# Weight products in one six-bank round and one joined to the scores; the last output tile in two column halves

## Chip, cores, metric

One core of a Trainium2 chip. The metric is the device time of one launch in microseconds (us), as the median of several executions. The profile is one execution with every instruction recorded. The engines are PE (TensorE matmul), PEld (its weight loads), DVE (VectorE), ACT (ScalarE), POOL (GpSimd) and SP (which issues DMAs).

## The reference

Eight batches of eight heads, 576 tokens, head size 64, 32 memory slots. Softmax-weighted sums of keys and values over the tokens give 32 memories per head, each token attends to those 32, and the result, `x` of 4608 x 512, goes through a gated feed-forward block.

```python
k_m = einsum('bhsm,bhsd->bhmd', a, k)        # a = softmax of phi over the tokens
v_m = einsum('bhsm,bhsd->bhmd', a, v)
attn = softmax(q @ k_m^T / sqrt(64))
x = (attn @ v_m), heads side by side          # 4608 x 512
out = (silu(x @ w_gate) * (x @ w_val)) @ w_out   # 512 -> 1536 -> 512
```

## The kernel before

It never forms `x`. It multiplies the value memories with the gate and value weights first: `U = v_m @ W`, per batch two kinds (gate 0, value 1) in three chunks `c` of 512 columns, each in two head groups. Then `x @ W` is `attn @ U`. One batch runs through these stages:

1. `scores` (on PE split into eight tiles of 64 rows x 32 columns, written 64*32), exponentials on ACT, sums and their inverse (`z_inv`), normalised tile `A` on DVE (`norm`);
2. 24 slots `gv_slot`: gate product, silu on ACT, value product, multiplication on DVE;
3. among those slots: output matmuls of the batches before (the "backlog", one unit = one 128x512 matmul), the key/value sums of the next batch (`kv_items`), and rounds of `U`.

In this program a bank is one PSUM buffer of up to 128 x 512 FP32: PE writes a product there, and the bank is free again when ACT or DVE has copied it.

```python
ps = ctx.enter_context(tc.tile_pool(name="ps", bufs=6, space=bass.MemoryType.PSUM))  # general banks
po = ctx.enter_context(tc.tile_pool(name="po", bufs=2, space=bass.MemoryType.PSUM))  # output matmuls

def u_round(b, parts, evac):                   # one bank per kind, chunk and group
    banks = []
    for which, c, halves in parts:
        ...
        for i in range(NP):
            for g in range(NG):
                nc.tensor.matmul(              # 64 rows x 32 columns: 8 tiles at once
                    p[g][32 * i:32 * i + 32, f0:f1],
                    lhsT=kTs[b][64 * g:64 * g + 64, 2, 32 * i:32 * i + 32],
                    rhs=W[which, c][64 * g:64 * g + 64, halves[0]:halves[-1] + 1, i],
                    start=True, stop=True, tile_position=(64 * g, 32 * i))
        ...
    for (t, p), e in zip(banks, evac):         # copies to SBUF: "a" on ACT, "v" on DVE
        ...

for b in range(2, B):                          # cut to what matters
    run(take(2))                               # 2 output matmuls
    for g in range(NG):
        scores(b, g)
    if b == 2:
        load_k(3); load_v(3); load_q(4); load_phi(4, nc.gpsimd)
    run(take(8))
    ...                                        # z_inv, 14 output matmuls, norm
    if b == 2:
        run(take(4))
        run([u_item(2, 0)] + take(6) + [u_item(2, 1)])
    run(take(12))
    # slots, spread over 0..24, with the rest of the backlog, and:
    #   b == 2: ([lambda: load_qT(3)], 12, 12)      q transposed by a DMA on SP
    #   (kv_items(b + 1, lambda: (u_item(b, 2)(), run(take(2)))), 9, 14)
    #   ([u_item(b + 1, 0)], 15, 17)
    #   ([u_item(b + 1, 1)], 21, 23)
    # and the loads, all on POOL's queue, in this order:
    #   load_q(b + 3), load_k(b + 2), load_v(b + 2), load_phi(b + 3)
```

A `u_item(b, c)` is one round of four banks: both kinds of chunk `c`, 16 matmuls in two waves of eight. A round with 128*128 matmuls on both sides is called solo.

The softmax here doesn't subtract the row's maximum and nothing guards it: scores larger than these inputs give would overflow.

Of the kernel before, what the change touches and what calls it, by code (L numbers as in the profile page):

```python
# [9 lines left out]
FP32 = mybir.dt.float32  # L10
# [4 lines left out]
def kernel(  # L15
# [17 lines left out]
    nc = tc.nc  # L33
# [3 lines left out]
    B, H, S, D = q.shape  # L37
    M = phi.shape[3]
    DM, DF = moe_w_gate.shape
# [3 lines left out]
    NJF = DF // 128  # L43
# [11 lines left out]
    work = ctx.enter_context(tc.tile_pool(name="work", bufs=3))  # L55
    ps = ctx.enter_context(tc.tile_pool(name="ps", bufs=6, space=bass.MemoryType.PSUM))
    po = ctx.enter_context(tc.tile_pool(name="po", bufs=2, space=bass.MemoryType.PSUM))
# [3 lines left out]
    out_r = out.rearrange("(b p j) c -> b j p c", b=B, p=P, j=J)  # L61
# [10 lines left out]
    def load_k(b):  # L72
        t = inp.tile([P, 2, H, J * D], BF16, tag="kv", name="t_kv")
        nc.gpsimd.dma_start(out=t[:, 0], in_=k[b].rearrange("h (p j) d -> p h (j d)", p=P))
        kvs[b] = t
# [20 lines left out]
    def load_qT(b):  # L96

        t = att.tile([128, H, 3, P], BF16, tag="qT", name="t_qT")
        nc.sync.dma_start_transpose(
            out=t.rearrange("p h j t -> p (h j) t"),  # L100
            in_=qs[b].rearrange("p h f -> p (h f)"),
        )
        for i in range(NP):
            qTs[b, i] = t[:, 2 * i:2 * i + 2].rearrange("p h j t -> p h (j t)")
# [18 lines left out]
    WO = {}  # L123
# [18 lines left out]
    def phi_exp(b):  # L142
        t = att.tile([P, J, NG, NP, M], BF16, tag="ephi", name="t_ephi")
        src = phis.pop(b).rearrange("p (i g) (j m) -> p g i j m", g=NG, m=M)
        for g in range(NG):
            nc.scalar.activation(  # L146
                out=t[:, :, g].rearrange("p j i m -> p i j m"), in_=src[:, g], func=AF.Exp
            )
        ephis[b] = t
# [201 lines left out]
    def u_round(b, parts, evac):  # L351

        banks = []
        for which, c, halves in parts:
            f0, f1 = HC * halves[0], HC * (halves[-1] + 1)
            p = [ps.tile([128, CH], FP32, tag="b", name=f"p_u{g}") for g in range(NG)]
            for i in range(NP):
                for g in range(NG):
                    nc.tensor.matmul(  # L359
# [3 lines that stand above are left out]
                        start=True,  # L363
                        stop=True,
                        tile_position=(64 * g, 32 * i),
                    )
            for g in range(NG):
                if (b, which, c, g) not in Us:
                    Us[b, which, c, g] = upool.tile(
                        [128, CH], BF16, tag=f"U{which}{c}{g}", name="t_U"  # L370
                    )
                banks.append((Us[b, which, c, g][:, f0:f1], p[g][:, f0:f1]))
        for (t, p), e in zip(banks, evac):
            if e == "a":
                nc.scalar.copy(out=t, in_=p)  # L375
            else:
                nc.vector.tensor_copy(out=t, in_=p)  # L377


    hts = {}  # L380
    pend = []

    def flush_mul():
        while pend:
            pend.pop(0)()
# [44 lines left out]
    def token_segments(t0, count):  # L430
        segs = []
        t = t0
        while t < t0 + count:
            bb, rest = divmod(t, S)
            blk, pp = divmod(rest, P)
            n = min(P - pp, t0 + count - t)
            segs.append((t - t0, n, bb, 2 * (blk % 3) + blk // 3, pp))
            t += n
        return segs

    def out_units(c, u, eng):

        mine = {}

        def unit(jf):
            def run():
                if jf == 0:
                    mine["p"] = po.tile([128, DM], FP32, tag="o", name="p_oo")
                nc.tensor.matmul(  # L449
                    mine["p"],  # L450
                    lhsT=hts[c, jf][:, 128 * u:128 * (u + 1)],
                    rhs=WO[jf],
                    start=(jf == 0),
                    stop=(jf == NJF - 1),
                )
                if jf == NJF - 1:
                    h = DM // 2 if eng == "av" else DM
                    for n, e in enumerate(eng):
                        t_o = work.tile([128, h], FP32, tag="to", name="t_o")
                        c0 = n * h  # L460
                        if e == "a":
                            nc.scalar.copy(out=t_o, in_=mine["p"][:, c0:c0 + h])  # L462
                        else:
                            nc.vector.tensor_copy(out=t_o, in_=mine["p"][:, c0:c0 + h])  # L464
                        q_out = nc.scalar if eng == "av" and e == "a" else nc.sync
                        for (r0, m, bb, jj, pp) in token_segments(2 * c * S + 128 * u, 128):
                            q_out.dma_start(
                                out=out_r[bb, jj, pp:pp + m, c0:c0 + h], in_=t_o[r0:r0 + m, :]
                            )

            return run

        return [unit(jf) for jf in range(NJF)]

    def out_list(b):
        tiles = range(0, 4) if b % 2 == 0 else range(4, 9)
        res = []
        for n, u in enumerate(tiles):
            eng = "av" if b + 1 == B and u == tiles[-1] else "v" if n % 4 != 3 else "a"
            res += out_units(b // 2, u, eng)  # L480
        return res

    def q_items(b, evac):
# [4 lines left out]
    def u_item(b, c, evac="avav"):  # L488

        both = ((0, c, (0, 1)), (1, c, (0, 1)))  # L490
        return lambda: u_round(b, both, evac)
# [6 lines left out]
    def u_half(b, which, c, half, evac):  # L498
        return lambda: u_round(b, ((which, c, (half,)),), evac)

    def run(items):
        for x in items:
            x()
# [10 lines left out]
    def exp_tables():  # L514
        nc.scalar.preload_act_table_set("natural_log_exp_and_others")  # L515
# [102 lines left out]
    def take(n):  # L618
        nonlocal backlog
        n = max(0, min(n, len(backlog)))  # L620
        part, backlog = backlog[:n], backlog[n:]
        return part

    for b in range(2, B):
        last = b + 1 == B
        exp_tables()
        if b == 2:
            load_qT(2)
            phi_exp(2)
            run(take(28))  # L630
            run(kv_items(2)[:1] + take(6) + kv_items(2)[1:] + take(14))
        run(take(2))
        for g in range(NG):
            scores(b, g)
        if b == 2:
            load_k(3)
            load_v(3)
            load_q(4)
            load_phi(4, nc.gpsimd)
        run(take(8))  # L640
        if not last:
            phi_exp(b + 1)
        z_inv(b, 0)
        run(take(1))
        z_inv(b, 1)
        nc.scalar.preload_act_table_set("silu_and_others")
        run(take(13))
        norm(b, 0)
        norm(b, 1)
        if b == 2:  # L650
            run(take(4))
            run([u_item(2, 0)] + take(6) + [u_item(2, 1)])
        run(take(12))
        g = gv_slots(b)
        beside = 0 if last else 2
        outs = [lambda: run(take(1)) for _ in range(len(backlog) - beside)]
        streams = [(g, 0, 24), (outs, 0, 24)]
        if last:
            streams += [([u_item(b, 2)], 5, 6)]
        if b == 2:  # L660
            streams += [
                ([lambda: load_qT(3)], 12, 12),
                (kv_items(3, lambda: (u_item(2, 2)(), run(take(2)))), 10, 14),
                ([u_item(3, 0)], 15, 17),
                ([u_item(3, 1)], 21, 23),
            ]
        elif not last:
            load_qT(b + 1)
        if not last:
            if b > 2:  # L670
                phi_sum(b + 1)
            if b + 3 < B:
                load_q(b + 3)
            if b + 2 < B:
                load_k(b + 2)
                load_v(b + 2)
            if b + 3 < B:
                load_phi(b + 3, nc.gpsimd)
        if not last and b > 2:
            streams += [  # L680
                (kv_items(b + 1, lambda: (u_item(b, 2)(), run(take(2)))), 9, 14),
                ([u_item(b + 1, 0)], 15, 17),
                ([u_item(b + 1, 1)], 21, 23),
            ]
        spread(*streams)
        flush_mul()
        backlog += out_list(b)
# [29 lines left out]
```

## Time and profile before

| | before |
|---|---|
| time, median | 252.27 us (252.22 to 252.77, 3 runs) |
| span of the profiled run | 249.9 us |
| PE busy | 241.4 us, 97% |
| last matmul ends, last store lands | 245.44, 248.58 |

The durations that the profile gives for matmuls overlap their successors, so distances here are taken from start to start. The lines themselves stand in the prediction.

### The profile page before, as it was taken

The page shows a single profiled execution, that of the slowest core. Times are in us where ns is not written, and L with a number is a line of the kernel's source. Part 1 is how long each engine was busy: PE and PEld are TensorE (multiplying, and loading weights), DVE is VectorE, ACT ScalarE, POOL GpSimd, SP SyncE. Part 2 cuts the span into 40 slices and gives each one's busy share as a digit, 9 for nine tenths or more (in the row PEclk, how much of TensorE's full clock was granted, in tenths as well). Part 3 has the DMA queues.
Part 4 walks back from the last instruction along what each step waited for, and adds up shares of the span by engine and source line. Part 5 has one row for each costly group of instructions (what it writes and reads, how often), then busy time and mean ns, then how long its engine had stood idle before and what let it go on. Part 6 is the DMA issues. An engine that isn't in the chain of part 4 may idle for free.

```text
span 249.9 us, 6646 instructions
## 1 busy us (share of the span) xinstructions
PE 241.4 (97%) x2610; PEld 149.6 (60%) x2610; DVE 153.7 (61%) x334; ACT 167.9 (67%) x365; POOL 54.4 (22%) x85
## 2 busy tenths in 40 slices
PE   7999799999999999999999999999999999999992
PEld 7976467674543765466645665476646664567540
DVE  0027689993318689378927786478826775587320
ACT  2459689885095768966896668866896669677200
POOL 8433365000050004072205320090007000000000
PEclk9999999999999999999999999999999999999998
DMA  7999999999699995994995499489236211310243
GB/s 180 205 203 201 198 197 202 232 213 172 140 171 250 239 195 70 216 288 85 178 256 133 79 176 230 123 158 160 41 80 145 55 24 43 86 42 3 57 113 84
DMA packets 49167, 37.00 MB, mean 148 GB/s; under 512 B 15984, under 2 KB 43888, under 8 KB 49136
## 3 DMA queue, kind: packets, MB, share of 16 engines
q0 software_dynamic: 27632, 22.42, 56.8%
q1 hardware_dynamic: 20560, 13.44, 23.2%
q10 hardware_dynamic: 944, 0.72, 1.1%
q8 instruction: 20, 0.33, 0.5%
q14 instruction: 11, 0.09, 0.1%
HBM read 42.47 MB, written 9.44 MB: 208 GB/s over the span
## 4 chain that ended last, share of the span: by engine, by line
PE 93%; ACT 3%; DVE 2%; DMA 1%; issue 0%
PE p_oo L449 37%; PE p_g L393 20%; PE p_v L393 19%; PE p_u L359 5%; PE p_oo L524 5%; PE p_kv L177 2%; PE p_g L316 1%; PE p_g L336 1%; PE p_v L336 1%; DMA out_dram<-t_o 1%; PE p_kv L197 1%; ACT L595 1%; ACT t_qT L303 0%; PE p_q L292 0%; ACT t_o L462 0%; PE p_T L241 0%
## 5 line engine op out<-in xcount | busy, mean ns | idle before, releaser
L449 PE MATMUL p_oo<-WO,t_h 128*128 128x512 bf16 x432 | 113.0, 379 | 0.0
L409 ACT ACTIVATE t_sg<-p_g 128x288 bf16<-128x288 f32 x192 | 77.7, 414 | 32.5 <-PE p_g L393 25.2
L416 DVE TENSOR_TENSOR t_h<-t_sg,p_v 128x288 bf16<-128x288 bf16 x192 | 84.6, 452 | 22.3 <-PE p_v L393 18.4
L393 PEld LDWEIGHTS <-t_U 128*128 128x128 bf16 x768 | 73.4, 98 | 33.9 <-issue 4.4
L393 PE MATMUL p_g<-t_A,t_U 128*128 128x288 bf16 x384 | 78.4, 286 | 1.0 <-ACT t_U L375 1.0
L393 PE MATMUL p_v<-t_A,t_U 128*128 128x288 bf16 x384 | 77.2, 286 | 0.0
L449 PEld LDWEIGHTS <-t_h 128*128 128x128 bf16 x432 | 41.1, 98 | 41.5 <-issue 4.7
L464 DVE COPY t_o<-p_oo 128x512 f32<-128x512 f32 (+1 forms) x28 | 19.1, 681 | 47.1 <-PE p_oo L449 40.0
L375 ACT CAST t_U<-p_u 128x512 bf16<-128x512 f32 (+1 forms) x52 | 26.2, 556 | 11.4 <-PE p_u L359 11.2
L377 DVE CAST t_U<-p_u 128x512 bf16<-128x512 f32 (+1 forms) x52 | 31.1, 642 | 0.8 <-PE p_u L359 0.5
L462 ACT COPY t_o<-p_oo 128x512 f32<-128x512 f32 (+1 forms) x9 | 5.1, 571 | 21.6 <-DMA out_dram<-t_o 11.3
L524 PE MATMUL p_oo<-bones 128*128 128x128 bf16 x218 | 16.0, 236 | 1.5 <-DVE bones L536 1.5
L93 POOL DMA_DIRECT2D t_q<-in_q_dram x6 | 4.7, 780 | 58.4 <-DMA t_qT<-t_q 57.6
L359 PE MATMUL p_u<-W,t_kT 64*32 64x512 bf16 (+1 forms) x416 | 15.6, 365 | 0.7 <-DVE t_kT L243 0.7
L524 PEld LDWEIGHTS <-bones 128*128 128x128 bf16 x218 | 14.4, 107 | 2.2 <-DVE bones L536 1.5
L146 ACT ACTIVATE t_ephi<-t_phi 96x768 bf16<-96x768 f32 x16 | 12.5, 845 | 4.2 <-DMA t_phi<-in_phi_dram 4.2
L160 POOL COPY t_mark<-t_A 1x1 bf16<-1x1 bf16 x4 | 0.7, 180 | 58.0 <-DVE t_A L345 58.0
L345 DVE TENSOR_TENSOR t_A<-t_E,t_lz 128x576 bf16<-128x576 bf16 x16 | 11.5, 750 | 0.4 <-ACT t_lz L340 0.4
L207 DVE RECIPROCAL t_rS<-p_kv 128x2 f32<-128x2 f32 x8 | 1.4, 170 | 16.5 <-PE p_kv L197 13.1
L340 ACT ACTIVATE t_lz<-t_lz 128x576 f32<-128x576 f32 x16 | 10.9, 683 | 0.5
L164 POOL TENSOR_TENSOR t_es<-t_es,t_ephi 96x256 f32<-96x256 f32 x16 | 10.7, 666 | 1.3
L515 ACT ACT_TABLE_LOAD x7 | 9.0, 1283 | 1.3 <-PEq L701 1.2
(49 smaller groups left out, 145.5 us busy)
## 6 DMA issues: line engine op xcount, KB each, us to landing
t_kv<-in_k_dram POOLq DMA_DIRECT2D x8, 576.0 KB, 9.5
t_kv<-in_v_dram POOLq DMA_DIRECT2D x8, 576.0 KB, 13.7
out_dram<-t_o SPq DMA_DIRECT2D x23, 192.0 KB, 2.6
t_phi<-in_phi_dram POOLq DMA_DIRECT2D x6, 576.0 KB, 14.8
t_q<-in_q_dram POOLq DMA_DIRECT2D x6, 576.0 KB, 8.1
out_dram<-t_o SPq DMA_DIRECT2D x24, 128.0 KB, 2.4
W<-in_moe_w_gate_dram POOLq DMA_DIRECT2D x6, 256.0 KB, 13.1
W<-in_moe_w_val_dram POOLq DMA_DIRECT2D x6, 256.0 KB, 12.8
```

Source lines behind the costliest of these rows:

```text
L146: nc.scalar.activation(out=t[:, :, g].rearrange("p j i m -> p i j m"), in_=src[:, g], func=AF.Exp)
L340: nc.scalar.activation(out=lz, in_=lz, func=AF.Exp, scale=-1.0)
L345: nc.vector.tensor_tensor(out=a, in0=es.pop((b, g)), in1=lzs.pop((b, g)), op=ALU.mult)
L359: nc.tensor.matmul(p[g][32 * i:32 * i + 32, f0:f1], lhsT=kTs[b][64 * g:64 * g + 64, 2, 32 * i:32 * i + 32], rhs=W[which, c][64 * g:64 * g ...
L375: nc.scalar.copy(out=t, in_=p)
L377: nc.vector.tensor_copy(out=t, in_=p)
L393: nc.tensor.matmul(p[:, 0:HALF], lhsT=Us[b, which, c, g][:, 128 * o:128 * (o + 1)], rhs=atts[b, g][:, r], start=(g == 0), stop=(g == NG - 1),)
L409: nc.scalar.activation(out=sg, in_=gate, func=AF.Silu)
L416: nc.vector.tensor_tensor(out=dst, in0=sg, in1=val, op=ALU.mult)
L449: nc.tensor.matmul(mine["p"], lhsT=hts[c, jf][:, 128 * u:128 * (u + 1)], rhs=WO[jf], start=(jf == 0), stop=(jf == NJF - 1),)
L464: nc.vector.tensor_copy(out=t_o, in_=mine["p"][:, c0:c0 + h])
L524: nc.tensor.matmul(p[:, 0:128], lhsT=bones, rhs=bones, start=True, stop=True)
```

## The change

Intent: fewer passages of PE between its full-size form and small tiles (one passage is a way into the 64*32 tiles and back out to 128*128). The rounds of chunks 0 and 1 become one round of six banks (chunk 0 of both kinds, chunk 1 of the gate) and one of two banks that runs directly before the scores, which use the same tiles. The last output tile is computed as two halves of 256 columns, each in a bank of its own, so that the first half's copy and stores run while PE computes the second.

```diff
+    def out_units_end(c, u):          # last tile: 2 halves, 12 matmuls of 256 columns each
+        ...
+                    nc.scalar.copy(out=t_o, in_=mine["p"])
+                    segs = token_segments(2 * c * S + 128 * u, 128)
+                    for n, (r0, m, bb, jj, pp) in enumerate(segs):
+                        (nc.sync, nc.scalar)[n % 2].dma_start(...)   # 32 rows on SP, 96 on ACT
+    def u_three(b):
+        u_round(b, ((0, 0, (0, 1)), (1, 0, (0, 1)), (0, 1, (0, 1))), "avavav")
+    def u_values(b):
+        u_round(b, ((1, 1, (0, 1)),), "vv")
...
-        run(take(2))
+        run(take(4))
+        u_values(b)
         for g in range(NG):
             scores(b, g)
...
-        run(take(8))
+        run(take(6))
...
-            run([u_item(2, 0)] + take(6) + [u_item(2, 1)])
+            u_three(2)
...
-        beside = 0 if last else 2
+        beside = 0 if last else 7
...
-                ([u_item(b + 1, 0)], 15, 17),
-                ([u_item(b + 1, 1)], 21, 23),
+                ([lambda: (run(take(2)), u_three(b + 1), run(take(3)))], 17, 18),
```

More of the change, by code (lines that the diff above doesn't have):

```diff
@@ L456, in run @@
                 if jf == NJF - 1:
-                    h = DM // 2 if eng == "av" else DM
-                    for n, e in enumerate(eng):
-                        t_o = work.tile([128, h], FP32, tag="to", name="t_o")
-                        c0 = n * h
-                        if e == "a":
-                            nc.scalar.copy(out=t_o, in_=mine["p"][:, c0:c0 + h])
-                        else:
-                            nc.vector.tensor_copy(out=t_o, in_=mine["p"][:, c0:c0 + h])
-                        q_out = nc.scalar if eng == "av" and e == "a" else nc.sync
-                        for (r0, m, bb, jj, pp) in token_segments(2 * c * S + 128 * u, 128):
-                            q_out.dma_start(
-                                out=out_r[bb, jj, pp:pp + m, c0:c0 + h], in_=t_o[r0:r0 + m, :]
-                            )
+                    t_o = work.tile([128, DM], FP32, tag="to", name="t_o")
@@ L471, in unit, with run @@
+                    if eng == "a":
+                        nc.scalar.copy(out=t_o, in_=mine["p"])
+                    else:
+                        nc.vector.tensor_copy(out=t_o, in_=mine["p"])
+                    for (r0, m, bb, jj, pp) in token_segments(2 * c * S + 128 * u, 128):
+                        nc.sync.dma_start(
+                            out=out_r[bb, jj, pp:pp + m, :], in_=t_o[r0:r0 + m, :]
+                        )
             return run
         return [unit(jf) for jf in range(NJF)]
+    def out_units_end(c, u):
+        h = DM // 2
+        mine = {}
+        def unit(half, jf):
+            def run():
+                if jf == 0:
+                    mine["p"] = po.tile([128, h], FP32, tag="o", name="p_oo")
+                nc.tensor.matmul(
+                    mine["p"],
+                    lhsT=hts[c, jf][:, 128 * u:128 * (u + 1)],
+                    rhs=WO[jf][:, h * half:h * (half + 1)],
+                    start=(jf == 0),
+                    stop=(jf == NJF - 1),
+                )
+                if jf == NJF - 1:
+                    t_o = work.tile([128, h], FP32, tag="to", name="t_o")
+                    nc.scalar.copy(out=t_o, in_=mine["p"])
+                    segs = token_segments(2 * c * S + 128 * u, 128)
+                    for n, (r0, m, bb, jj, pp) in enumerate(segs):
+                        (nc.sync, nc.scalar)[n % 2].dma_start(
+                            out=out_r[bb, jj, pp:pp + m, h * half:h * (half + 1)],
+                            in_=t_o[r0:r0 + m, :],
+                        )
+            return run
+        return [unit(half, jf) for half in range(2) for jf in range(NJF)]
@@ L478, in out_list @@
         for n, u in enumerate(tiles):
-            eng = "av" if b + 1 == B and u == tiles[-1] else "v" if n % 4 != 3 else "a"
-            res += out_units(b // 2, u, eng)
+            if b + 1 == B and u == tiles[-1]:
+                res += out_units_end(b // 2, u)
+            else:
+                res += out_units(b // 2, u, "v" if n % 4 != 3 else "a")
         return res
@@ L663 @@
                 (kv_items(3, lambda: (u_item(2, 2)(), run(take(2)))), 10, 14),
-                ([u_item(3, 0)], 15, 17),
-                ([u_item(3, 1)], 21, 23),
+                ([lambda: (run(take(2)), u_three(3), run(take(3)))], 17, 18),
             ]
```

## The prediction

> **What bounds the kernel now.** I read the page first (busy shares, the chain that ended last), then the groups, then the timeline of PE around the weight-product rounds, then all engines from one batch's scores to its next products, and last the end.
>
> ```profile
> PE 241.4 (97%) x2610; PEld 149.6 (60%) x2610; DVE 153.7 (61%) x334; ACT 167.9 (67%) x365; POOL 54.4 (22%) x85
> PE 93%; ACT 3%; DVE 2%; DMA 1%; issue 0%
> L449 PE MATMUL p_oo<-WO,t_h 128*128 128x512 bf16 x432 | 113.0, 379 | 0.0
> L359 PE MATMUL p_u<-W,t_kT 64*32 64x512 bf16 (+1 forms) x416 | 15.6, 365 | 0.7 <-DVE t_kT L243 0.7
> PEld L359 <- issue: 5.2, 19, 0.4
> ```
>
> TensorE is busy 97% of 249.9 us and is 93% of the chain, with almost no named wait, so only work or empty array time taken off PE's own stream, or off the tail, can shorten the run. The durations of the groups overlap, so I use starts. 25 output matmuls (128x512) take 5.40 us from start to start of the next kind, 0.216 each; a 128x288 product takes 0.1225. The last line says that weight loads of L359 sat 0.3 to 0.4 us behind nothing that the profile names. The timeline of PE at one such round shows what that is:
>
> ```profile
> 118.44 0.38 PE L449 MATMUL p_oo<-WO,t_h 128*128 128x512 bf16 x1
> 118.74 0.62 PE L359 MATMUL p_u<-W,t_kT 64*32 64x512 bf16 x16
> 119.30 0.42 PE L393 MATMUL p_g<-t_A,t_U 128*128 128x288 bf16 x2
> 119.56 0.41 PE L393 MATMUL p_v<-t_A,t_U 128*128 128x288 bf16 x2
> 119.85 0.41 PE L393 MATMUL p_g<-t_A,t_U 128*128 128x288 bf16 x2
> ```
>
> The output matmul should give way after 0.216 and does so after 0.30: 0.09 is lost going into 64*32 tiles. The round's 16 matmuls run on eight tiles in two waves; in the single records the waves begin at 118.744 and 118.971, 0.227 apart, yet the second is followed only after 0.330: 0.10 is lost coming out. All solo rounds after 55 us read alike (0.558 us long, entry 0.087). Also, 119.56 to 119.85 is 0.29 where two products take 0.245: a 0.05 wait for a bank that ACT is still emptying.
>
> **What the Trainium skill says.** "TensorEngine Tiling (Array Packing)", Key Properties: "Changing tiling mode (not just tile) drains the TensorE". The trace agrees: 0.09 in, 0.10 out, and nothing between two waves of one mode. "TensorE: Matmul & The Clock Gate", in the section that explains 56 ns, gives N ÷ 2.4 GHz plus about 2.5 ns per warm matmul: 215.7 ns at 512, which is the trace's 0.216; for 256 columns my estimate from it is 109 ns. "PSUM — Partial Sum Buffer", the section on bank collisions, says two engines may not read one bank in the same partitions at once; at the end, DVE's half copy starts at 245.885, just after ACT's ended at 245.853, so this order is kept here. "DMA: Bandwidth & Descriptors", Anatomy of one DMA, puts the fixed part at about 2.0 us (for the path through GpSimd); the last four stores, from SP and ACT, land 1.5 to 2.1 us after issue.
>
> **The change, part by part: (1) rounds.** For each batch from 2 to 7, two solo rounds of two waves (W chunks 0 and 1, both kinds) become one round of three waves (six banks) and one wave put directly before the scores, which use the same 64*32 tiles. Waves stay at four; the solo rounds fall from two to one. Fixed part of a solo round: 0.087 + 0.558 - 2 x 0.227 = 0.191 us. Six batches: 6 x 0.191 = 1.15 us less on PE, which is the path. The third round (chunk 2, behind the key/value sums) stays.
>
> **(2) small bank waits.** Single starts show 0.05 after the round at 118.74 and again at 173.7; 0.05 in the scores at 125.36 and 180.3; 0.06 at 127.97 and 182.9: 0.32 us in all. The six-bank round is followed by three output matmuls (0.65 us), which use other banks, and the late round of chunk 1 is gone from before the scores. I count 0.2 as gained.
>
> **(3) evacuation.** The copies are as many as before: 128x512 on ACT 0.54 apart, on DVE 0.64. Per batch ACT does one fewer and DVE one more in total, but two of DVE's move to just after the scores, where DVE was idle 2.7 us before its next copy. In the product stretch, DVE's tightest (15.4 of 18.0 us busy at 107.4 to 125.4), each has one fewer. No cost.
>
> **(4) the order around the scores.**
>
> ```profile
> 124.83 0.59 PE L449 MATMUL p_oo<-WO,t_h 128*128 128x512 bf16 x2
> 125.50 1.28 ACT L515 ACT_TABLE_LOAD   x1
> 125.78 1.90 PE L449 MATMUL p_oo<-WO,t_h 128*128 128x512 bf16 x8
> 126.79 0.41 ACT L326 ACTIVATE t_E<-p_g 128x288 bf16<-128x288 f32 x1
> 131.90 1.42 DVE L345 TENSOR_TENSOR t_A<-t_E,t_lz 128x576 bf16<-128x576 bf16 x2
> 133.68 0.41 PE L393 MATMUL p_g<-t_A,t_U 128*128 128x288 bf16 x2
> ```
>
> Four output matmuls and one wave now come ahead of the scores instead of two output matmuls: the first scores start some 0.43 + 0.23 = 0.66 later. Their reader, the exponential at 126.79, waits for ACT's table load and not for the scores, done by 125.78: 1.0 us of room. Without the late U casts, ACT can reach the load no later. The output matmuls behind the scores are two fewer, so PE comes to the next products at the same total plus the wave that came in; the normalised tile was ready at 133.32 against 133.68. No cost expected.
>
> **(5) the end.**
>
> ```profile
> 235.78 9.66 PE L449 MATMUL p_oo<-WO,t_h 128*128 128x512 bf16 x44
> 245.48 0.37 ACT L462 COPY t_o<-p_oo 128x256 f32<-128x256 f32 x1 [2.00 <-DMA out_dram<-t_o]
> 245.88 0.81 ACTq L467 DMA_DIRECT2D out_dram<-t_o  x2
> 245.88 0.42 DVE L464 COPY t_o<-p_oo 128x256 f32<-128x256 f32 x1 [4.89 <-ACT t_o L462]
> ```
>
> The wait named DMA is really the last matmul, which ends at 245.44. Then ACT 0.37, DVE 0.42, SP issues the 32 rows at 246.34 and the 96 rows at 246.71, which land at 248.58; closing takes 1.30 more. Afterwards 12 matmuls of 0.216 become 24 of 0.109 (+0.03), the first half's copy and stores hide behind the second half's 1.31 us of matmuls, and the second half needs one copy (0.37) and one issue on each of two queues: issue near 245.91 on the old clock. ACT's 96-row store took 2.08 and SP's 1.87; with 2.0, it lands near 247.9, 0.65 before 248.58. I take 0.6 after the 0.03.
>
> **Sum.** 1.15 + 0.2 + 0.6 = 1.95 us less: 252.27 - 1.95 = 250.3 us. Clock and DMA do not change.
>
> **Rivals. (A) Six banks starve the products.** All six general banks belong to the round at once. Counting from its first wave: DVE's three casts end near 1.18, 1.82, 2.46 (in the old round DVE starts 0.54 after the first matmul), ACT's at 1.0, 1.54, 2.07. PE, after three waves (0.785) and three output matmuls, is back at 1.43 and asks for a bank every 0.245: 1.43, 1.68, 1.92, 2.17, 2.41, 2.66 in the same order. Every one is free 0.2 us or more ahead, but a lag of 0.5 on DVE eats it: +0.3 in five batches, 251.8. Against it: two output matmuls stand before the round too, and batch 3's DVE lag, about 0.6 after the key/value copies, is nearly gone by then. **(B) The exponential chain becomes the wait.** If the scores, not the table load, set it, products start some 0.2 late in six batches: 251.5. The 1.0 us of room speaks against. **(C) The drain is per wave, not per switch**, so a third wave or a second kind of operand costs its own 0.1: half of (1) is lost, 250.9. The 0.227 between two waves in one mode speaks against. **(D) The tail does not move**, because two stores at once land later: 250.8; the old end had the same four stores within 0.9 us and landed each within 2.1.
>
> **Range and chances.** The middle is my sum; A and C in part give the upper side, a larger relief of waits (all 0.32) and a tail gain of 0.8 the lower. 8 in 10: 249.6 to 251.2. Faster by over 2% needs 5.0 us, over twice all I can find: 0.01. Slower by over 2% needs a new stall of 7 us: 0.01. Within 2%: 0.98.
>
> **What would show it.** Right: in PE's timeline a round of 24 matmuls about 0.79 long, another of 8 followed by the scores with no output matmul and no gap between, entries still 0.09; the start of the key/value sums of the last batches moved up by 0.2 per batch; between the last matmul and the last landing about 2.5 us instead of 3.14. Wrong: over 0.1 of idle at the products after a six-bank round (A), at the first product of a batch (B), waves in one mode further apart than 0.23 (C), stores landing 2.5 us or more after issue (D). More than one of these at full size makes the prediction wrong.

## The result

| | before | changed |
|---|---|---|
| time, median of 4 runs | 252.31 us | 249.78 us (249.41 to 249.98) |
| ratio | | 0.9894, interval 0.9877 to 0.9912 |
| span of the profiled run | 249.88 | 248.15 |
| first product of batch 3 after the first output matmul | 50.65 | 50.19 |
| first product of batch 3 to that of batch 4 | 26.26 | 25.87 |
| first product of batch 4 to that of batch 7 | 83.64 | 82.80 |
| that of batch 7 to the end of the last matmul | 28.12 | 28.16 |
| last matmul's end to the last landing | 3.14 | 2.49 |
| landing to the end of the span | 1.30 | 1.36 |

A ratio is the mean time of one kernel's fast runs over that of the other's in the same rounds, so not quite the ratio of the medians. In two later sets of runs of the changed kernel the ratio was 0.9906 both times (medians 249.75 and 249.81 against 251.91 and 252.06). The gain is thus 2.2 to 2.5 us where 1.95 was forecast. The intervals lie clear below 1; the gain is about 1%.

The distances of the table are the best ruler: between the first products of two batches both kernels have done exactly the same work, and the distances repeat to 0.01 us from execution to execution. Their differences, taken before rounding, are 0.46, 0.39, 0.84 and -0.03 on PE, sum 1.66, and 0.65 - 0.06 behind it: 2.25 us. The profiled span fell by only 1.73, because this execution came to its first key/value sum 0.5 us later (11.88 against 11.36), in code that the change does not touch. The traces show where: the 140 warm-up matmuls ahead of that sum start at 1.52 in all fourteen profiles and follow each other at 107 ns up to some moment, then at 56 ns. That moment was 5.44 in before and 6.51 in the changed kernel: ten more matmuls at the slow pace, 0.5 us. Over the fourteen profiles it lies between 4.7 and 7.2, just ahead of the trace's first record of a full clock (4.9 to 7.3), and the first sum follows it (11.0 to 12.2). The three profiles with the old rounds have early ones (11.0 to 11.4), but one with the new rounds has too (g2, 11.3), and the unprofiled runs show no later start: in the set of f4 below, eleven runs of before had spans of 249.7 to 250.5 (mean 250.0), five of the changed kernel 247.5 to 248.6 (mean 247.9), 2.1 us apart. So I take the moment for chance, which is not shown beyond that.

From the page of the changed kernel: busy time, the chain, the output matmuls.

```profile
PE 237.2 (96%) x2595; PEld 152.2 (61%) x2622; DVE 158.3 (64%) x339; ACT 166.0 (67%) x360; POOL 54.5 (22%) x85
...
PE 92%; ACT 3%; issue 2%; DVE 1%; DMA 1%
...
L449 PE MATMUL p_oo<-WO,t_h 128*128 128x512 bf16 x393 | 101.6, 379 | 3.0 <-issue 2.9
```

"issue 2%" and 3.0 us of idle are not waits. There are 2595 matmul records but 2622 weight loads; 35 tiles of 12 matmuls should give 420 records of L449, and 393 are there. The trace lost 27 records, 18 of them of the first full-size matmul behind a tiled section. Such a hole is 0.216 long and has no releaser; it must be subtracted before anything is read from the lines around it. In f4, the same program run again, no record is lost.

The timeline of PE of the changed kernel, the six-bank round and then the joined one of batch 5 (start, duration, engine, line):

```profile
146.63 0.59 PE L449 MATMUL p_oo<-WO,t_h 128*128 128x512 bf16 x2
147.16 0.84 PE L359 MATMUL p_u<-W,t_kT 64*32 64x512 bf16 x24
148.16 0.81 PE L449 MATMUL p_oo<-WO,t_h 128*128 128x512 bf16 x3 [0.16 <-issue]
...
152.85 1.03 PE L449 MATMUL p_oo<-WO,t_h 128*128 128x512 bf16 x4
153.81 0.41 PE L359 MATMUL p_u<-W,t_kT 64*32 64x512 bf16 x8
154.04 0.28 PE L316 MATMUL p_g<-t_qT,t_kT 64*32 64x288 bf16 x1
...
154.62 0.59 PE L449 MATMUL p_oo<-WO,t_h 128*128 128x512 bf16 x2 [0.16 <-issue]
```

147.16 to 148.16 is 1.00, less one lost record of 0.216: 0.784 for three waves, where 0.785 was forecast. The same round without a lost record, in f4:

```profile
120.00 0.84 PE L359 MATMUL p_u<-W,t_kT 64*32 64x512 bf16 x24
120.77 0.82 PE L449 MATMUL p_oo<-WO,t_h 128*128 128x512 bf16 x3
```

It takes 0.774 by the single records, so the third wave adds 0.216 to the 0.558 of two. The eight matmuls at 153.81 give way to the scores after 0.23 with nothing between: the passage is gone. In the line at 152.85, four matmuls should take 0.864 and take 0.96: the entry still costs 0.09.

The end of the changed kernel, all engines:

```profile
243.02 0.37 ACT L489 COPY t_o<-p_oo 128x256 f32<-128x256 f32 x1 [0.72 <-PE p_oo L480]
243.42 0.37 ACTq L492 DMA_DIRECT2D out_dram<-t_o  x1
...
244.34 0.37 ACT L489 COPY t_o<-p_oo 128x256 f32<-128x256 f32 x1 [0.95 <-DMA out_dram<-t_o]
244.74 0.38 ACTq L492 DMA_DIRECT2D out_dram<-t_o  x1
```

The first half is copied and issued while PE works on; behind the last matmul (244.29) stand one copy and one issue. (The wait of the last copy, named DMA, is for that matmul, as it was in the kernel before.) ACT's 96-row store, issued at 244.74, lands at 246.79.

### The profile page after: what moved, and what is told of

It reads as the page before. It is cut to its first block, busy times and chain, and to the rows that moved or that the text cites. A ratio compares the mean times of both kernels' runs of the same rounds, so it can differ in the third digit from the quotient of the medians.

```text
span 248.2 us, 6645 instructions
## 1 busy us (share of the span) xinstructions
PE 237.2 (96%) x2595; PEld 152.2 (61%) x2622; DVE 158.3 (64%) x339; ACT 166.0 (67%) x360; POOL 54.5 (22%) x85
## 4 chain that ended last, share of the span: by engine, by line
PE 92%; ACT 3%; issue 2%; DVE 1%; DMA 1%
PE p_oo L449 35%; PE p_g L393 20%; PE p_v L393 19%; PE p_u L359 5%; PE p_oo L560 5%; PE p_kv L177 2%; PE p_g L316 1%; PE p_g L336 1%; DMA out_dram<-t_o 1%; PE p_v L336 1%; PE p_kv L197 1%; ACT L631 1%; ACT t_qT L303 0%; PE p_q L292 0%; PE p_T L241 0%
## 5 line engine op out<-in xcount | busy, mean ns | idle before, releaser
L449 PE MATMUL p_oo<-WO,t_h 128*128 128x512 bf16 x393 | 101.6, 379 | 3.0 <-issue 2.9
L449 PEld LDWEIGHTS <-t_h 128*128 128x128 bf16 x420 | 39.6, 98 | 41.0 <-issue 6.0
L377 DVE CAST t_U<-p_u 128x512 bf16<-128x512 f32 (+1 forms) x58 | 34.8, 646 | 7.3 <-PE p_u L359 7.3
L461 DVE COPY t_o<-p_oo 128x512 f32<-128x512 f32 x27 | 18.6, 690 | 31.4 <-PE p_oo L449 31.3
L375 ACT CAST t_U<-p_u 128x512 bf16<-128x512 f32 (+1 forms) x46 | 22.7, 554 | 10.8 <-PE p_u L359 10.6
L560 PE MATMUL p_oo<-bones 128*128 128x128 bf16 x218 | 16.6, 240 | 1.5 <-DVE bones L572 1.5
L459 ACT COPY t_o<-p_oo 128x512 f32<-128x512 f32 x8 | 4.7, 588 | 19.7 <-PE p_oo L449 19.5
L560 PEld LDWEIGHTS <-bones 128*128 128x128 bf16 x218 | 14.9, 109 | 2.3 <-DVE bones L572 1.5
L340 ACT ACTIVATE t_lz<-t_lz 128x576 f32<-128x576 f32 x16 | 10.9, 683 | 0.5
L359 PEld LDWEIGHTS <-t_kT 64*32 64x32 bf16 x416 | 4.8, 89 | 9.5 <-issue 7.0
```

Source lines behind the costliest of these rows:

```text
L340: nc.scalar.activation(out=lz, in_=lz, func=AF.Exp, scale=-1.0)
L359: nc.tensor.matmul(p[g][32 * i:32 * i + 32, f0:f1], lhsT=kTs[b][64 * g:64 * g + 64, 2, 32 * i:32 * i + 32], rhs=W[which, c][64 * g:64 * g ...
L375: nc.scalar.copy(out=t, in_=p)
L377: nc.vector.tensor_copy(out=t, in_=p)
L449: nc.tensor.matmul(mine["p"], lhsT=hts[c, jf][:, 128 * u:128 * (u + 1)], rhs=WO[jf], start=(jf == 0), stop=(jf == NJF - 1),)
L461: nc.vector.tensor_copy(out=t_o, in_=mine["p"])
```

## Experiments

Theory T: the gain is the passages into and out of the small tiles (one less per batch), small bank waits, and the end. Rivals: R1, the gain is in relieved copies and banks, not in passages; R2, the end's gain is chance; R3, six banks at once cost something hidden. All runs were correct, and all executions but one were fast: one of the eleven of before in the third set took 314.54 us at a clock of 0.756, and the ratios leave it out.

| run | median us | ratio to before | interval |
|---|---|---|---|
| e1_tail_only | 251.30 | 0.9970 | 0.9956 to 0.9984 |
| e2_rounds_only | 250.57 | 0.9942 | 0.9927 to 0.9958 |
| e3_values_solo | 251.20 | 0.9960 | 0.9946 to 0.9974 |
| e4_split_three | 252.30 | 1.0004 | 0.9989 to 1.0018 |
| f1_no_cover | 250.76 | 0.9950 | 0.9938 to 0.9962 |
| f2_one_queue | 250.40 | 0.9938 | 0.9921 to 0.9955 |
| f3_tail_384 | 249.71 | 0.9914 | 0.9900 to 0.9928 |
| f4_after_again | 249.75 | 0.9906 | 0.9892 to 0.9919 |
| g1_kv_first | 251.47 | 0.9988 | 0.9954 to 1.0023 |
| g2_after_third | 249.81 | 0.9906 | 0.9890 to 0.9923 |
| g3_kv_late | 255.52 | 1.0127 | 1.0093 to 1.0162 |
| g4_kv_late_before | 252.30 | 1.0017 | 0.9991 to 1.0042 |

Before had medians of 251.98 (e), 251.91 (f) and 252.06 (g).

### Each half of the change alone: e1 and e2

e1 is the kernel before with only the hunk of the last tile; e2 is the changed kernel with the last tile's code of before.

> Only the last output tile is changed, all rounds stay as before. Theory (the end is worth 0.6 us: from the last matmul to the last landing 2.5 us in place of 3.14, closing 1.3 to 1.4): 251.7 against 252.3, ratio 0.9976. Rival (the profile's 0.6 at the end is an accident of one execution, the stores land later in most): ratio 0.999 to 1.000 and over 3 us from the last matmul to the last landing.

> Only the rounds are changed, the last tile stays as before. Theory (six solo rounds less at 0.2 us each, plus the 0.32 us of bank waits that are gone, plus about 0.1 of first matmuls after a drain): 1.7 us less, 250.6, ratio 0.9933; the distance between the first products of batches 4 and 7 is 108.7 us in place of 109.9. Rival (the profile of the changed kernel began 0.5 us later than that of before by accident, so its true gain on PE is over 2 us): ratio 0.991 or lower.

e1: the PE distances are those of before (26.26 and 83.64), and from last matmul to landing it took 2.46 us. R2 falls; the other eight profiles with this same end have 2.48 to 2.51. e2: 25.87 and 82.80, together 108.67, as expected (108.7 in place of 109.9; the expectation wrote "batches 4 and 7" for 3 and 7), and its end took 3.56, with an SP store that landed 2.3 us after issue where before it was 1.87. The two ratios multiply to 0.9912, the later ratios of the whole are 0.9906: the parts add up, and no hidden third part is needed. The rival of e2, that more than 2 us came from PE, is refuted by the distances.

### One passage more, twelve more: e3 and e4

```diff
 # e3
-        run(take(4))
+        run(take(2))
         u_values(b)
+        run(take(2))
         for g in range(NG):
             scores(b, g)
 # e4: u_three as three rounds of two banks, one output matmul between, taken from those behind
+        u_round(b, ((0, 0, (0, 1)),), "av")
+        run(take(1))
+        u_round(b, ((1, 0, (0, 1)),), "av")
+        run(take(1))
+        u_round(b, ((0, 1, (0, 1)),), "av")
```

> The changed kernel, with the four output matmuls ahead of the single round set as two, round, two, scores: same instructions, same counts, one more passage out of and into the small tiles in each of six batches. Theory (the gain is the drains): 6 x 0.2 = 1.2 us of the gain are lost, near 250.9, ratio to before 0.994; in the records the solo round takes about 0.33 to its follower and both entries 0.087. Rival (the gain comes from relieved copies and bank waits, not from the joining): the time of the changed kernel, ratio 0.989 to 0.990.

> The changed kernel, with its six-bank round cut into three solo rounds of one wave, one output matmul between each (taken from those around it): twice two more passages in each of six batches. Theory: 12 x 0.2 = 2.4 us more than the changed kernel, near 252.1, ratio to before 0.999. Rival (six banks at once cost hidden waits that the split would relieve, or the cost is per wave and already paid): no slower than the changed kernel, ratio 0.987 to 0.990.

The timeline of PE of e3, to be set beside 152.85 to 154.62 above:

```profile
153.56 0.59 PE L449 MATMUL p_oo<-WO,t_h 128*128 128x512 bf16 x2
154.08 0.41 PE L359 MATMUL p_u<-W,t_kT 64*32 64x512 bf16 x8
154.42 0.60 PE L449 MATMUL p_oo<-WO,t_h 128*128 128x512 bf16 x2
154.96 0.29 PE L316 MATMUL p_g<-t_qT,t_kT 64*32 64x288 bf16 x1
```

The same eight matmuls now occupy PE for 0.34 in place of 0.23, and the scores have an entry of their own to pay, 0.10, beside the 0.09 ahead of the round that the changed kernel pays too. With scores that are 0.01 longer these are all the differences between the two traces from batch 4 to 7: per batch 0.116 + 0.103 + 0.009. Against the changed kernel, batch 4 to 7 grew from 82.80 to 83.48 (three passages more: 0.23 each), in e4 to 84.17 (six more: 1.37, again 0.23 each). Over the whole stretch from the first output matmul, e3 lost 1.37 us and e4 2.75: 0.23 for each of 6 and of 12. Doubling the cause doubles the cost. R1 keeps little: e3 has the same instructions and the same number of copies and lost 1.4 us of median. With as many passages as before, it is still 0.32 us ahead of before on PE (160.23 against 160.55 from the first output matmul to the first product of batch 7); that much is bank waits. R3 falls for this kernel: smaller rounds did not help. The ratio of e3, 0.996, is above the 0.994 expected: that started from the first set's ratio for the change (0.9894, later 0.9906) and from 0.2 for a passage.

### The cover behind the six-bank round: f1

```diff
-                ([lambda: (run(take(2)), u_three(b + 1), run(take(3)))], 17, 18),
+                ([lambda: (run(take(5)), u_three(b + 1))], 17, 18),
```

> The changed kernel, with the three output matmuls behind the six-bank round put before it (five before, none behind), in the five rounds that stand among the products. Theory (the drain sum only holds because the copies hide behind them): PE asks for banks 0.65 us sooner, waits about 0.3 for the first and some 0.5 in all per round, 2 to 2.5 us more, near 252.0, ratio to before 0.998 to 1.000. Rival (the order of output matmuls is of no account, the copies are fast enough): the time of the changed kernel, ratio 0.990.

The timeline of PE of f1 behind a six-bank round:

```profile
120.07 0.84 PE L359 MATMUL p_u<-W,t_kT 64*32 64x512 bf16 x24
121.18 0.41 PE L393 MATMUL p_g<-t_A,t_U 128*128 128x288 bf16 x2 [0.27 <-ACT t_U L375]
```

The first bank is waited for as worked out (0.27 where about 0.3 was expected), but the later ones hardly: the slots of an odd batch lost 0.39 us (25.87 became 26.26), those of an even one, where an output matmul of the slots still follows the round, 0.10; 1.1 us in all, and 1.0 in the median. The expected 2 to 2.5 was twice too much. My reading, not tested, is that the first wait delays all later requests, so that most banks are free by then. The three output matmuls behind the round are worth 1 us.

### The end: f2 and f3

f2 issues all four stores of the last tile on SP (`nc.sync.dma_start` in place of the pair). f3 cuts the tile into 384 and 128 columns, the 128 copied by DVE.

> The changed kernel, with all four stores of the last tile issued by SP, so that the last half's 96-row store is issued after the 32-row one. Theory (half of the 0.6 at the end is the second queue): last landing some 0.3 later, from the last matmul to the last landing 2.8 us in place of 2.5. Rival (the second bank alone gives the gain, the queues contend anyway): 2.5 us.

> The changed kernel, with the last tile cut into 384 and 128 columns in place of 256 and 256, the 128 copied by DVE. Theory: the last copy shrinks from 0.37 to about 0.22, issue and landing stay, 0.15 us less from the last matmul to the last landing (2.35), invisible in the time. Rival (the stores of the larger piece still occupy the queues): 2.5 us or more.

The end of f2, SP's issues and the last copy:

```profile
244.29 2.37 SPq L492 DMA_DIRECT2D out_dram<-t_o  x4
245.14 0.37 ACT L489 COPY t_o<-p_oo 128x256 f32<-128x256 f32 x1 [0.98 <-DMA out_dram<-t_o]
```

With one queue, SP is still issuing the first half's stores (until 245.73) when the second half's copy ends at 245.51, and its last store is issued at 246.25 and lands at 248.10: 3.04 us behind the last matmul, where the changed kernel has 2.49 and before 3.14. So with one queue the two banks gain only 0.10 at the end, with two queues 0.65; the 0.55 between them is more than the 0.3 expected. But the second queue is not new: the kernel before used both too, one for each half (ACTq and SP in the prediction's lines and text). What the change itself took away is read from the starts of both traces. Before, the last 96 rows waited for the second copy (0.45) and for SP's issue of the 32 rows (0.37); in the changed kernel both are gone from their way, and their store took 0.17 longer: 0.65. f3 is a miss: the 128-column copy took 0.29 in place of 0.37, but its store landed 2.17 us after issue in place of 2.05, and the distance was 2.53. It beats nothing.

### A wait that comes and goes: f4

> The changed kernel once more, beside the other runs of this call. Theory (sum of the measured parts, 0.23 for each of six passages, 0.32 of bank waits, 0.6 at the end, together 2.3): 249.8, ratio 0.991. If the ratio is 0.989 or lower again, 0.3 us are still without a cause; 11.9 us at the first key/value sum, as in four of six profiles, would mean that the start is longer with the change and not by accident.

The ratio confirms the sum. But in this execution batch 3 to 4 took 26.60 us and not 25.87. In f2 it was 26.35, in f3 26.09, all with the rounds of the changed kernel. PE's timeline in f4:

```profile
112.27 0.24 PE L197 MATMUL p_kv<-ones,t_ehl 96*128 96x1 bf16 x4
113.17 0.85 PE L177 MATMUL p_kv<-t_kv,t_ephi 96*32 96x128 bf16 x48 [0.66 <-DMA t_kv<-in_v_dram]
```

The sums of batch 4 wait for the load of V. I had not thought of it: in the profile of before V lands at 109.59 and the sums start at 113.11, 3.5 us of room. In that of the changed kernel V lands at 112.66 and the sums start at 112.73. The queues show why. First before, SP then POOL, then the changed kernel in the same order:

```profile
83.15 1.11 SPq L467 DMA_DIRECT2D out_dram<-t_o  x2
84.37 6.69 SPq L99 DMA_TRANSPOSE t_qT<-t_q  x1
```

```profile
95.80 0.77 POOL L93 DMA_DIRECT2D t_q<-in_q_dram  x1 [23.34 <-DMA t_qT<-t_q]
...
97.32 0.77 POOL L78 DMA_DIRECT2D t_kv<-in_v_dram  x1
```

```profile
89.33 1.13 SPq L463 DMA_DIRECT2D out_dram<-t_o  x2
90.57 3.34 SPq L99 DMA_TRANSPOSE t_qT<-t_q  x1
```

```profile
97.83 0.77 POOL L93 DMA_DIRECT2D t_q<-in_q_dram  x1 [25.54 <-DMA t_qT<-t_q]
...
99.35 0.77 POOL L78 DMA_DIRECT2D t_kv<-in_v_dram  x1
```

In batch 2 the change puts six output matmuls fewer ahead of the slots (88 in place of 94 by the weight loads), so an output tile is copied 6.2 us later (88.70 against 82.54 in the records); its stores are issued later; the transposition of q, next in SP's queue, is issued at 90.57 in place of 84.37; the next load of q may only overwrite when that has landed; and K and V of batch 4 stand behind that load. Not all of the 6.2 us arrives: that transposition takes 6.7 us to land in place of 10.9, so the loads are issued 2.0 us later, and V lands 3.1 later. Four queue positions turn a reordering of matmuls into a later load, while PE itself arrives earlier. Three of the six profiles with the changed rounds (changed, e2, g2 without; f3, f2, f4 with) show the wait, of 0.2, 0.5 and 0.7 us.

### Moving that load: g1, g3, g4

```diff
 # g1: K and V ahead of q
-            if b + 3 < B:
-                load_q(b + 3)
             if b + 2 < B:
                 load_k(b + 2)
                 load_v(b + 2)
             if b + 3 < B:
+                load_q(b + 3)
                 load_phi(b + 3, nc.gpsimd)
 # g3 (changed kernel) and g4 (kernel before), for b == 2: q, phi, then K, V
```

> The changed kernel, with the loads of each batch's K and V issued ahead of the load of q instead of behind it, so that they don't wait for the transposition of q that stands behind an output store. Theory (since the change V of batch 4 lands at the moment its sums are due, and in some executions PE waits 0.2 to 0.7 us for it): V of batch 4 lands before 110, no wait of the sums for V, 25.9 us between the first products of batches 3 and 4 (26.1, 26.4 and 26.6 in the runs with a wait), some 0.3 us less than the changed kernel in the mean, 249.4. Rival (the wait is of the DMA engines being full, whatever the order): V lands as late, same time as the changed kernel.

> The changed kernel beside the one with K and V first: 249.75, ratio 0.991; PE waits between 0 and 0.7 us for V of batch 4.

> The changed kernel, with K and V of batch 4 issued after both q and phi. Theory (V of batch 4 is at the edge in the changed kernel): V lands near 115 in place of 112.7, PE waits 2.0 to 2.4 us, near 251.8, ratio 0.999. Rival (there is room before the sums): no change, 249.8.

> The kernel before, with K and V of batch 4 issued after both q and phi. Theory (before the change V landed 3.5 us ahead of its sums, phi takes about 2.2): V lands near 111.8, the sums at 113.1 don't wait, ratio 1.000. Rival (the order matters as much in the old kernel): 2 us slower, ratio 1.008.

g4 against g3 shows the edge: the same later order costs the kernel before nothing (V at 112.61, sums at 113.00, batch 3 to 4 26.25), and the changed one 5.7 us of median. The mechanism of g3 was expected, its size was not: V landed at 116.64, so PE waited 4.0 us, and then its clock fell. The windows of g3 (columns: busy us and number of each engine, granted PE clock, DMA share, GB/s):

```profile
116.60:119.30 2.70, 2.46 (x64) 1.49 (x66) 1.06 (x4) 0.52 (x2) 0.32 (x1) 0.50 0.61 137
119.30:122.20 2.90, 2.72 (x10) 1.52 (x10) 1.44 (x4) 1.38 (x4) 2.79 (x4) 0.50 0.54 51
122.20:125.00 2.80, 2.80 (x25) 2.21 (x24) 2.21 (x6) 1.72 (x5) 0.00 (x0) 0.96 1.30 200
```

For 5.6 us after the wait the clock was half, which can cost up to 2.8 us. Batch 3 to 4 took 32.65, 6.8 above 25.87: about 4.0 of waiting, and the rest slow clock. The Trainium skill's page "TensorE: Matmul & The Clock Gate", Part 1, states half rate after an idle window of about 3.4 us. The trace agrees in kind: by its clock records the half rate began at 115.62, 3.0 us after the last matmul had ended (112.67), and lasted to 122.45. The waits under 1 us show nothing of the kind.

g1 did its part and failed: K and V landed by 97.5, batch 3 to 4 was 25.87. But PE lost 1.3 us elsewhere, as its waits between 79 and 109 us show (us in total, times, longest):

```profile
PE p_g L316 <- DMA t_qT<-t_q: 1.1, 1, 1.1
```

K and V were now read while the transposition of q for batch 3 was on its way (DMA share 1.41 in place of 0.54 between 90 and 99 us). That transposition took 6.08 us to issue in place of 3.34, and the scores of batch 3 waited for it. That the reads slowed it is my reading; no run isolates it. The order of loads only chose which load was on the edge. What remains untried is to issue the transposition ahead of the output store on SP. No version tried beats the changed kernel.

## Why the prediction was right, and where its steps were off

- **Passages (1.15 forecast).** Right in kind, low in size: 0.191 was read from the gaps around one round; e3 and e4 measured 0.23, so 6 x 0.23 = 1.37. The traces show the missing 0.04: the entry is 0.093 in every solo round of before and not 0.087; a wave behind others costs 0.216 (third wave, f4) and not the 0.227 that I took twice; and the first product behind a round takes 0.133 and not 0.1225, which I had left out. 0.093 + 0.558 - 2 x 0.216 + 0.01 is 0.23.
- **Bank waits (0.2 of 0.32 taken).** All were gained: 1.37 + 0.32 = 1.69 is the whole of the 0.46 + 0.39 + 0.84 measured, and e3 shows the 0.32 by itself. My discount was for nothing.
- **Copies and the order around the scores (no cost).** Right: no stage shows a wait at its first product, and the distances of later stages have no rest.
- **The end (0.6, after 0.03 for the smaller matmuls).** Right: 0.65 at the landing, 0.06 lost in the closing, PE 0.03 longer. The mechanism was right too: one copy and one issue left the path (0.45 + 0.37), less 0.17 for a slower store; the 256-column matmuls follow each other at 0.109, as estimated. What I had not seen is how much of it needs both queues (f2).
- **Rivals.** A (six banks starve the products) did not occur, and f1 shows that it would without the three covering matmuls: 1.1 us, not the 2 to 2.5 that I then worked out. B did not occur. C, cost per wave, is refuted by the 0.774 for three waves. D is refuted by e1; its sign did show once, a store of the first half that took 2.62 us to land, but off the path: it was down 0.64 before the last one.
- **"Clock and DMA do not change."** Wrong: I compared PE, ACT and DVE through the reordering and not SP's and POOL's queues, where the last 3.5 us of room for V of batch 4 went. It costs up to 0.7 us in half of the profiles, which the larger gain on PE covers.

Together: 1.95 forecast, plus 0.22 for the passages and 0.12 for the bank waits, less 0.04 at the end, is the 2.25 of the profiles without a wait for V; the medians of the three sets say 2.2 to 2.5. The wait for V takes some 0.2 of it on average of the six profiles.

## What to carry to other kernels

When PE is always busy, read the distance from start to start around each change of its tile form: the cost here is per passage, not per wave, so join sections of one form and leave real work on other banks behind a round that takes all banks. At the end of this kernel the issue time of stores is on the path: giving up the second queue cost 0.55 us (f2), and a last copy shorter by 0.08 gained nothing (f3). After moving work in one engine's program, follow the DMA queues too: a store that moves back pulls along everything behind it in its queue.

## What the Trainium skill lacked or had wrong

- "TensorEngine Tiling (Array Packing)", Key Properties, states the drain and no cost: 0.23 us for each extra section of small tiles (e3 and e4), of which 0.09 to 0.10 is the entry and about 0.12 the way out.
- "Trainium Kernel Development and Optimization", Key Constraints, says that issuing from several engines only saves the sequencer's issue time. That is borne out and can be much: 0.55 us at the end of a 250 us kernel (f2, with one queue, against the changed kernel, with two), as one queue takes 0.3 to 0.9 us per store.
- No page read warns that matmul records can be missing right behind a tiled section: 27 of 2622 in the changed kernel, 18 of them there, each shown as 0.16 of idle time without a cause; none in f4, the same program.
- "TensorE: Matmul & The Clock Gate", Part 1, gives about 3.4 us for the idle window before half rate; in g3 the half rate came 3.0 us after the last matmul's end.
